# Grouped 1x1 convolution: one in-place ring in slots of 128 columns, with register addresses on TensorE

## The chip, the cores and the metric

The kernel runs on one core of a Trainium2 chip. The metric is device time in microseconds, from the first to the last instruction of one execution with what the launch adds around it. A profile is one execution recorded by the chip's profiler; its times are its own.

## What is computed

An image of 512 x 512 pixels has 192 channels in bf16, in 4 groups of 48. Each pixel's 48 channels of a group are multiplied by that group's 48 x 48 matrix; the kernel size is 1 and there is no padding.

```
H = W = 512; G = 4; Cg = 48; C = 192; k = 1
x: (1, 512, 512, 192) bf16        w: (1, 1, 4, 48, 48) bf16
out = einsum('bhwgc,gcd->bhwgd', x.reshape(B, H, W, G, Cg), w[0, 0])
return out.reshape(B, H, W, C)
```

The input is 100.66 MB and so is the output; both go through DMA once.

## The kernel before, in words

**Tiling.** The pixels are laid over the 128 partitions of SBUF, so that a *column* is one pixel of each partition, 192 channels or 384 bytes of a partition's row. Four columns are a *group*, two groups a *pair*. The plan makes 529 groups in 265 pairs.

**Pieces.** `plan_pieces` cuts the columns into slots of 64 (`SLOT`); the first slot is cut further into pieces of 8, 24 and 32 (`HEAD`). Two slots (`SHARED_AT`) are *shared* pieces that fill only 60 of the 128 partitions, so that one of the 16 DMA engines has less to move: 16 partitions go by the ordinary queues and 44 by GpSimd's. There are two rings in SBUF, `xin` and `xout`, of 256 columns each (four slots).

**Engines.** SyncE issues the transfer of the weights (L231) and then the load of each piece (L235), waiting before each until TensorE is done with the columns that it overwrites (`groups_before`, counted on `mm_done`). GpSimd builds an identity and a selection matrix, issues the shared pieces' second part (L204, L206; the small `cur` transfers turn its DMA engines round to the right one), and announces each landed piece to TensorE by adding its pairs to `ready` (L219). TensorE builds a block weight matrix from ten small matmuls (L247), which VectorE casts to `wt` (L306). Then for each pair it does 12 transposes (L261: six blocks of 128 x 128 per group, the input block being the operand that a weight load brings in and the identity the one that streams) and, one pair behind, 12 matmuls (L276) of the transposed data with `wt`. VectorE copies the transposes of a pair from PSUM to SBUF in one copy of 128 x 1536 (L312). ScalarE evicts each group's result to `xout` (L346, 128 x 768, f32 to bf16), waits first until the store that used these columns has landed, and issues the stores (L332) when a piece is complete; the last nine slots are stored in halves or quarters.

**Order on TensorE.** The order is written out by hand: transposes of pair j + 1, then matmuls of pair j. The matmuls wait for VectorE's copy by a semaphore step of the sequencer (L269, `e_left`) and, at the first matmul of each group, for an eviction of two groups earlier (`o_left`), since PSUM holds two groups of results. The loop (`Fori`, L288) has 64 groups in its body, as many as `xin` holds, so that every address is a constant. It turns 8 times; nine pairs follow it. At the end of a turn three semaphore steps (L292 to L294) lower the counters by one lap, and then an addition to the loop register and a branch follow (both L288). VectorE has a loop of the same length.

## Time and profile before

| what | us |
|---|---|
| three timed runs | 476.95, 484.16, 486.12 (median 484.16) |
| the profiled execution | 476.64, of it span 474.5 |
| TensorE busy (matmul, weight load) | 436.9, 394.1 |
| ScalarE busy | 398.4, of it 529 evictions at 802 ns |
| VectorE busy | 254.1 |
| data moved in the span | 201.53 MB, 425 GB/s in the mean |
| granted TensorE clock, mean | 0.981 |

Busy time of an engine is not its bound by itself: an engine can be busy nearly all the time at the pace of another. In the profile, PE is TensorE's matmul side and PEld its weight loads; a name with q (SPq, PEq, PEldq) is an engine's sequencer, for steps that use no datapath. `out<-in` names the tensors written and read. Idle time stands in brackets with what ended it; "issue" is idle time for which the profile shows no cause outside the engine.

### The profile page before, as it was taken

The numbers are of one execution on the slowest core, as the hardware profiler recorded it, in microseconds if no ns is written. First come the engines' busy times: TensorE is split into PE (matmuls) and PEld (weight loads), VectorE is DVE, ScalarE is ACT, GpSimd is POOL, SyncE is SP. The second block draws the span as 40 slices with busy tenths as digits, with TensorE's granted clock in tenths as the row PEclk, the third lists the DMA queues.
The fourth block names the chain that finished last, engine by engine and source line by source line (L and its number), as shares of the span: only waits on it lengthen the run. The fifth ranks groups of instructions, "written<-read, shape, count | busy, mean of one in ns | idle before, by whom it ended". The sixth has DMA issues, their size and how long they took to land.

```text
span 474.5 us, 14050 instructions
## 1 busy us (share of the span) xinstructions
PE 436.9 (92%) x6358; PEld 394.1 (83%) x6358; DVE 254.1 (54%) x266; ACT 398.4 (84%) x530; POOL 5.9 (1%) x16
## 2 busy tenths in 40 slices
PE   4999999999999999999889859999989999999970
PEld 4988988988989889898779759898879898988860
DVE  2556555555555555555555535555555555555540
ACT  2899989998999989998888848999879998998880
POOL 1000100000000000000000000000000000000000
PEclk9999999999999999999999979999999999999995
DMA  8999999999999999999999999999999999999998
GB/s 329 427 406 432 431 428 433 431 431 429 429 429 432 429 431 429 431 429 431 429 434 429 437 433 433 435 431 433 429 430 435 431 422 433 431 431 421 427 426 334
DMA packets 11981, 201.53 MB, mean 425 GB/s; under 512 B 1744, under 2 KB 2000, under 8 KB 2640
## 3 DMA queue, kind: packets, MB, share of 16 engines
q1 hardware_dynamic: 5144, 98.52, 48.6%
q10 hardware_dynamic: 6376, 98.50, 48.6%
q0 software_dynamic: 448, 4.33, 2.2%
q8 instruction: 8, 0.13, 0.1%
q14 instruction: 5, 0.04, 0.0%
HBM read 100.68 MB, written 100.66 MB: 424 GB/s over the span
## 4 chain that ended last, share of the span: by engine, by line
PE 56%; DMA 39%; ACT 1%; issue 1%; SPq 0%; POOLq 0%; ACTq 0%
PE o_ps L276 33%; PE xT_ps L261 23%; DMA xin<-in_x_dram 20%; DMA out_dram<-xout 18%; ACT xout L346 1%; SPq L235 0%; SPq L231 0%; POOLq L219 0%; ACTq L51 0%
## 5 line engine op out<-in xcount | busy, mean ns | idle before, releaser
L346 ACT CAST xout<-o_ps 128x768 bf16<-128x768 f32 x529 | 397.1, 802 | 62.1 <-PE o_ps L276 51.0
L312 DVE COPY xT_sb<-xT_ps 128x1536 bf16<-128x1536 bf16 x265 | 253.4, 956 | 201.3 <-PE xT_ps L261 201.3
L276 PE MATMUL o_ps<-wt,xT_sb 128*128 128x144 bf16 (+1 forms) x3174 | 294.3, 234 | 6.8 <-ACT xout L346 2.7
L276 PEld LDWEIGHTS o_ps<-wt,xT_sb 128*128 128x128 bf16 x3174 | 212.8, 98 | 46.8 <-ACT xout L346 30.6
L261 PE MATMUL xT_ps<-ident,xin 128*128 128x128 bf16 x3174 | 223.5, 221 | 14.0 <-POOLq L219 12.7
L261 PEld LDWEIGHTS xT_ps<-ident,xin 128*128 128x128 bf16 x3174 | 192.2, 99 | 16.6 <-POOLq L219 14.1
L204 POOL DMA_DIRECT2D cur<-in_x_dram x4 | 2.3, 584 | 321.0 <-PE o_ps L276 162.0
L247 PE MATMUL o_ps<-w_sb,esel 48*128 48x48 bf16 x10 | 0.6, 210 | 2.7 <-DMA w_sb<-in_w_dram 2.7
L247 PEld LDWEIGHTS o_ps<-w_sb,esel 48*128 48x128 bf16 x10 | 0.5, 113 | 2.7 <-POOL esel L190 2.7
L306 DVE CAST wt<-o_ps 128x480 bf16<-128x480 f32 x1 | 0.7, 658 | 3.3 <-PE o_ps L247 3.3
L346 ACT ACT_TABLE_LOAD x1 | 1.3, 1283 | 0.8 <-PEq L367 0.8
L206 POOL DMA_DIRECT2D xin<-in_x_dram x2 | 1.1, 563 | 0.0
L206 POOL DMA_DIRECT2D out_dram<-xout x2 | 1.1, 562 | 0.0
L190 POOL TENSOR_SCALAR_AFFINE_SELECT esel<-esel 48x272 bf16<-48x272 bf16 x1 | 0.4, 402 | 0.0
L187 POOL MEMSET esel<- 48x272 bf16 x1 | 0.3, 318 | 0.3 <-POOLq L367 0.3
L194 POOL TENSOR_SCALAR_AFFINE_SELECT ident<-ident 128x128 bf16<-128x128 bf16 x1 | 0.3, 282 | 0.0
L188 POOL MEMSET ident<- 128x128 bf16 x1 | 0.2, 198 | 0.0
L367 POOL MEMSET const-float32-0.0<- 128x1 f32 x1 | 0.1, 98 | 0.3 <-issue 0.3
L367 POOL MEMSET const-bfloat16-1.0<- 128x1 bf16 x1 | 0.1, 101 | 0.0
L367 POOL MEMSET const-uint8-127<- 128x1 uint8 x1 | 0.1, 101 | 0.0
L367 POOL MEMSET const-float32-1.0<- 128x1 f32 x1 | 0.1, 98 | 0.0
## 6 DMA issues: line engine op xcount, KB each, us to landing
xin<-in_x_dram SPq DMA_DIRECT2D x30, 3072.0 KB, 35.3
out_dram<-xout ACTq DMA_DIRECT2D x22, 3072.0 KB, 32.7
out_dram<-xout ACTq DMA_DIRECT2D x15, 1536.0 KB, 33.5
out_dram<-xout ACTq DMA_DIRECT2D x2, 1152.0 KB, 17.5
xin<-in_x_dram POOLq DMA_DIRECT2D x2, 1056.0 KB, 19.9
out_dram<-xout POOLq DMA_DIRECT2D x2, 1056.0 KB, 19.3
xin<-in_x_dram SPq DMA_DIRECT2D x1, 1536.0 KB, 9.4
xin<-in_x_dram SPq DMA_DIRECT2D x3, 384.0 KB, 3.5
```

Source lines behind the costliest of these rows:

```text
L187: gp.memset(esel[:], 1.0).then_inc(p0_sem, 1)
L190: gp.affine_select(out=esel[:], in_=esel[:], pattern=[[-1, ECOLS]], compare_op=AluOpType.is_equal, fill=0.0, base=ESHIFT, channel_multipli ...
L194: gp.affine_select(out=ident[:], in_=ident[:], pattern=[[-1, 128]], compare_op=AluOpType.is_equal, fill=0.0, base=0, channel_multiplier=1) ...
L204: gp.dma_start(cur[0:turn, turns[0]], few).then_inc(cur_sem, 16)
L206: gp.dma_start(*((sbuf, dram) if inward else (dram, sbuf))).then_inc(done, 16)
L247: last = pe.matmul(o_ps[:, NOB - 1, col:col + CG], lhsT=esel[:, s0:s0 + 128], rhs=w_sb[:, g, :], start=True, stop=True, skip_group_check=True)
L261: last = pe.transpose(xT_ps[:, g % NXP, i * 128:(i + 1) * 128], xg[:, i * 128:(i + 1) * 128], ident[:])
L276: last = pe.matmul(o_ps[:, v % NOB, c0_:c1_], lhsT=xs[:, i * 128:(i + 1) * 128], rhs=wt[:, WOFF[tc]:WOFF[tc] + (c1_ - c0_)], start=(tc == ...
L306: dve.tensor_copy(wt[:], o_ps[:, NOB - 1, 0:WCOLS]).then_inc(wc_sem, 1)
L312: dve.tensor_copy(xT_sb[pair % NXS][:, 0:n * 2 * UC].rearrange("p (g c) -> p g c", g=n), xT_ps[:, b0:b0 + n, 0:2 * UC]).then_inc(e_left, 1)
L346: act.copy(dst, o_ps[:, v % NOB:v % NOB + 2, 0:UC]).then_inc(o_left, 1)
L367: nc = _bacc.Bacc("TRN2", target_bir_lowering=False, num_devices=1)
```

## The change

One ring takes the place of the two. `ring` holds 512 columns in four slots of 128; a group is loaded into it, and ScalarE evicts the result to the same columns, from which it is stored. A load therefore waits until the stores of a lap before have landed (`wait_free`, on SyncE and on GpSimd), and ScalarE no longer waits for stores. The ring is declared in bytes (`U8`) and its slices are read as bf16.

The first slot is cut into 8, 24, 32 and 64; the shared pieces are still 64 columns wide, each followed by an ordinary piece of 64. Only the last three slots are stored in parts. Full-width loads become 20 transfers and stores 25.

TensorE's loop covers one slot, 32 groups, and turns 16 times. As the slot changes from turn to turn, the address of each transposed block is a register: at the head of a turn the byte offsets of the slot and of the next one are computed (`here`, `there`), and for each of the 12 transposes of a pair the built program has a register addition (`RegisterAlu`) and then the transpose with the register as address. In the built loop body these are 194 register operations and 2 fused ones beside 384 transposes and matmuls. The nine pairs after the loop and the first pair before it have constant addresses, as before. VectorE's loop has 16 copies instead of 32.

SyncE issues the load of the first piece ahead of the transfer of the weights.

```diff
-SLOT = 64
-IN_COLS = 4 * SLOT
-OUT_COLS = 4 * SLOT
-HEAD = (8, 24, 32)
-LATE = 9
-LAST_PARTS = (24, 16, 12, 12)
-LOOP = IN_COLS // 4
-SHARED_AT = (6, 22)
+SLOT = 128
+COLS = 4 * SLOT
+COL = 2 * C
+HEAD = (8, 24, 32, 64)
+LATE = 3
+LAST_PARTS = (28, 16, 12, 12)
+LOOP = SLOT // 4
+SHARED_AT = (4, 10)
-AHEAD = IN_COLS // SLOT - 2
+WIDE = 64
+AHEAD = 1
...
-        xin = es.enter_context(nc.sbuf_tensor("xin", [128, IN_COLS * C], BF16))
-        xout = es.enter_context(nc.sbuf_tensor("xout", [128, OUT_COLS * C], BF16))
+        ring = es.enter_context(nc.sbuf_tensor("ring", [128, COLS * COL], U8))
...
+        def wait_stored(wq, i):
+            p = stores[i][0]
+            wq.wait(st_sem[i], 16 * len(p.on(SYNC)))
+            if p in pooled:
+                wq.wait(ps_sem[p], pool_val[p])
+
+        def wait_free(wq, p):
+            lap = COLS // 4
+            for i in sorted({store_of[g - lap] for g in range(p.g0, p.g1) if g >= lap}):
+                wait_stored(wq, i)
...
                 if ahead in pooled:
-                    wq.wait(mm_done, groups_before(ahead))
-                    pool_dmas(ahead, xf, xin, True, pl_sem[ahead])
+                    wait_free(wq, ahead)
+                    pool_dmas(ahead, xf, True, pl_sem[ahead])
...
-            sp.dma_start(w_sb[:], wv).then_inc(w_sem, 16)
             for p in pieces:
-                wq.wait(mm_done, groups_before(p))
-                for _, dram, sbuf in transfers(xf, xin, p, SYNC):
+                wait_free(wq, p)
+                for _, dram, sbuf in transfers(xf, p, SYNC):
                     sp.dma_start(sbuf, dram).then_inc(ld_sem[p.i], 16)
+                if p.i == 0:
+                    sp.dma_start(w_sb[:], wv).then_inc(w_sem, 16)
...
-                    xg = columns(xin, g)
-                    for ul in range(2):
-                        for tc in range(3):
-                            i = ul * 3 + tc
-                            last = pe.transpose(xT_ps[:, g % NXP, i * 128:(i + 1) * 128],
-                                                xg[:, i * 128:(i + 1) * 128], ident[:])
+                    for i in range(6):
+                        at = 4 * g % SLOT * COL + i * 256
+                        if base is None:
+                            xs = ring[:, 4 * g % COLS * COL + i * 256:][:, 0:256]
+                        else:
+                            xs = ring[:, bass.ds(base + at, 256)]
+                        last = pe.transpose(xT_ps[:, g % NXP, i * 128:(i + 1) * 128], xs.bitcast(BF16), ident[:])
...
-                with pe.Fori(0, turns_of_loop):
+                with pe.Fori(0, turns_of_loop) as turn:
+                    here = pe.snap((turn & 3) * (SLOT * COL))
+                    there = pe.snap(((turn + 1) & 3) * (SLOT * COL))
                     for j in range(LP):
-                        transposes(j + 1, range(2 * j + 2, 2 * j + 4))
+                        transposes(j + 1, range(2 * j + 2, 2 * j + 4), here if j + 1 < LP else there)
                         matmuls(j, range(2 * j, 2 * j + 2))
...
             for g in range(NG):
-                if g >= OUT_COLS // 4:
-                    wait_stored(store_of[g - OUT_COLS // 4])
                 wq.wait(mm_done, g + 1)
                 v = 2 * g
-                dst = columns(xout, g).rearrange("p (u c) -> p u c", u=2)
+                dst = columns(g).rearrange("p (u c) -> p u c", u=2)
```

More of the change, by code (lines that the diff above doesn't have):

```diff
@@ L8 @@
 F32 = mybir.dt.float32
+U8 = mybir.dt.uint8
 GROUPS = 4
@@ L23 @@
 ECOLS = 272
-SLOT = 64
-IN_COLS = 4 * SLOT
-OUT_COLS = 4 * SLOT
-HEAD = (8, 24, 32)
-LATE = 9
-LAST_PARTS = (24, 16, 12, 12)
-LOOP = IN_COLS // 4
-SHARED_AT = (6, 22)
+SLOT = 128
[6 more added lines that the diff above has]
+SHARED_AT = (4, 10)
 SYNC, POOL = 0, 1
-SHARED = ((0, 16, 4, SLOT, SYNC), (52, 44, 11, SLOT, POOL))
-AHEAD = IN_COLS // SLOT - 2
+WIDE = 64
+SHARED = ((0, 16, 4, WIDE, SYNC), (52, 44, 11, WIDE, POOL))
+AHEAD = 1
 NXP = 4
@@ L64, in __init__ @@
         self.i, self.slot, self.size = i, slot, size
-        self.at = {IN_COLS: 4 * g0 % IN_COLS, OUT_COLS: 4 * g0 % OUT_COLS}
+        self.at = 4 * g0 % COLS
         self.g0, self.g1 = g0, g0 + size // 4
@@ L72, in __init__ @@
         self.pix_end = pix
-        assert size % 4 == 0 and all(at + size <= cols for cols, at in self.at.items())
+        assert size % 4 == 0 and self.at + size <= COLS
     def on(self, queue):
@@ L88, in plan_pieces @@
         if n in at:
-            parts = [(SLOT, SHARED)]
+            parts = [(WIDE, SHARED), (SLOT - WIDE, None)]
         elif n == 0 and cols >= SLOT:
@@ L122, in groups, with span, transfers @@
         return range(2 * pair, min(2 * pair + 2, NG))
-    def transfers(ap, ring, p, queue, c0=0, c1=None):
-        at = p.at[ring.shape[1] // C]
+    def span(c0, c1, r0=0, r1=128):
+        return ring[r0:r1, c0 * COL:c1 * COL].bitcast(BF16)
+    def transfers(ap, p, queue, c0=0, c1=None):
+        at = p.at
         for b in p.on(queue):
@@ L132, in transfers @@
                 view = px.rearrange("(c a i) n -> a c (i n)", a=b.parts, c=b.rows // b.parts)
-            yield b, view, ring[b.r0:b.r0 + b.rows, (at + e0) * C:(at + e1) * C]
+            yield b, view, span(at + e0, at + e1, b.r0, b.r0 + b.rows)
     stores = []
@@ L139, in bass_standalone__grouped__vision_kernel @@
         parts = (p.size,)
-        if p.full and p.size == SLOT and late < LATE:
-            parts = LAST_PARTS if late == 1 else (p.size - half, half)
+        if p is pieces[-1] and p.size == sum(LAST_PARTS):
+            parts = LAST_PARTS
+        elif p.full and late < LATE and half:
+            parts = (p.size - half, half)
         c = 0
@@ L174, in bass_standalone__grouped__vision_kernel, with columns @@
         ready, e_left, o_left = sem("ready"), sem("e_left"), sem("o_left")
-        def columns(ring, g):
-            c = 4 * g % (ring.shape[1] // C)
-            return ring[:, c * C:(c + 4) * C]
-        def groups_before(p):
-            pairs = (p.g1 - LOOP + 1) // 2
-            return max(2 * pairs - 3, pairs > 0)
+        def columns(g):
+            c = 4 * g % COLS
+            return span(c, c + 4)
+        def wait_stored(wq, i):
[7 more added lines that the diff above has]
+                wait_stored(wq, i)
         @block.gpsimd
@@ L197, in _, with pool_dmas @@
             cursor, turns = [0], [0]
-            def pool_dmas(p, ap, ring, inward, done):
-                for b, dram, sbuf in transfers(ap, ring, p, POOL):
+            def pool_dmas(p, ap, inward, done):
+                for b, dram, sbuf in transfers(ap, p, POOL):
                     turn = (b.engine - cursor[0]) % 16
@@ L222, in _ @@
                     wq.wait(mm_done, q.g1 + 2)
-                    pool_dmas(q, of, xout, False, ps_sem[q])
+                    pool_dmas(q, of, False, ps_sem[q])
             for p in pooled:
@@ L249, in build_weights, with transposes @@
                 last.then_inc(wb_sem, 1)
-            def transposes(j, gs):
+            def transposes(j, gs, base=None):
                 if j % LP in starts:
@@ L296, in _ @@
             for j in range(NP - first[0]):
-                g0 = 2 * first[0]
                 if j + 1 < NP - first[0]:
-                    transposes(j + 1, [g - g0 for g in groups(first[0] + j + 1)])
-                matmuls(j, [g - g0 for g in groups(first[0] + j)])
+                    transposes(j + 1, groups(first[0] + j + 1))
+                matmuls(j, [g - 2 * first[0] for g in groups(first[0] + j)])
         @block.vector
@@ L330, in store @@
                 p, c0, c1, g1 = todo.pop(0)
-                for _, dram, sbuf in transfers(of, xout, p, SYNC, c0, c1):
+                for _, dram, sbuf in transfers(of, p, SYNC, c0, c1):
                     act.dma_start(dram, sbuf).then_inc(st_sem[i], 16)
-            def wait_stored(i):
-                p = stores[i][0]
-                wq.wait(st_sem[i], 16 * len(p.on(SYNC)))
-                if p in pooled:
-                    wq.wait(ps_sem[p], pool_val[p])
             for g in range(NG):
-                if g >= OUT_COLS // 4:
-                    wait_stored(store_of[g - OUT_COLS // 4])
                 wq.wait(mm_done, g + 1)
                 v = 2 * g
-                dst = columns(xout, g).rearrange("p (u c) -> p u c", u=2)
+                dst = columns(g).rearrange("p (u c) -> p u c", u=2)
                 act.copy(dst, o_ps[:, v % NOB:v % NOB + 2, 0:UC]).then_inc(o_left, 1)
@@ L352, in _ @@
             for i in range(len(stores)):
-                wait_stored(i)
+                wait_stored(wq, i)
 _INS = ['x', 'w']
```

## The prediction, made before the changed kernel ran

> **What bounds the kernel now.** I read the page first (busy shares, slices, DMA queues), then the groups by line, the waits, SyncE's waits, the table by stage, and last the timeline around one back edge of TensorE's loop.

> ```profile
> PE 436.9 (92%) x6358; PEld 394.1 (83%) x6358; DVE 254.1 (54%) x266; ACT 398.4 (84%) x530; POOL 5.9 (1%) x16
> ...
> DMA  8999999999999999999999999999999999999998
> ...
> q1 hardware_dynamic: 5144, 98.52, 48.6%
> q10 hardware_dynamic: 6376, 98.50, 48.6%
> q0 software_dynamic: 448, 4.33, 2.2%
> ```

> The three data queues' packets take 48.6 + 48.6 + 2.2 = 99.4% of what 16 DMA engines have in the span: 472 of 474.5 us. Transfers are the bound from end to end; neither end has more than some 2 us of slack. But TensorE (92%) and ScalarE (84%) stand close behind.

> ```profile
> 60.00:230.00 170.00, 167.03 (x2461) 150.73 (x2459) 98.47 (x103) 153.78 (x206) 1.10 (x2) 1.00 1.00 430
> 230.00:290.00 60.00, 50.99 (x721) 45.75 (x719) 28.49 (x30) 44.84 (x61) 1.10 (x2) 0.94 1.00 431
> ```

> Columns: stretch, its length, busy us of PE, PEld, DVE, ACT, POOL, clock, DMA share, GB/s. From 60 to 230 us TensorE runs without a stall: 103 VectorE copies (one per pair of groups) in 170 us, 1.65 us a pair, working off what loads had brought early. After 230 us it waits for loads. So compute's own pace is 1.63 to 1.65 us a pair, while the DMA engines allow 472/265 = 1.78. The whole reserve of compute is about 0.13 us a pair, 34 us over 265 pairs.

> ```profile
> PEld o_ps L276 <- ACT xout L346: 30.6, 130, 0.2
> PE xT_ps L261 <- POOLq L219: 12.7, 7, 4.9
> ACT xout L346 <- DMA out_dram<-xout: 2.9, 2, 2.3
> ```

> The pace of 1.63 is ScalarE's: in every second group a weight load waits for an eviction. Now the place where TensorE's sequencer does steps of its own, between two turns of the loop:

> ```profile
> 167.68 0.39 PEld L276 LDWEIGHTS o_ps<-wt,xT_sb 128*128 128x128 bf16 x6 [0.24 <-ACT xout L346]
> 168.51 0.67 PEld L261 LDWEIGHTS xT_ps<-ident,xin 128*128 128x128 bf16 x12 [0.45 <-issue]
> ```
> ```profile
> L288 PEldq ALU_OP  x8: 36/36/42, 62.2 to 445.9; - x8
> L288 PEldq COMPARE_BRANCH  x8: 76/208/235, 62.4 to 446.0; - x8
> ```

> Between those weight loads stand three semaphore steps (L292 to L294), one ALU_OP and one branch: 0.83 us from the load that ScalarE released to the first transpose, five steps that TensorE could not hide. In the trace's records of this edge the three semaphore steps start 150 ns apart, the ALU_OP's successor 97 ns after it (97 to 102 over the eight turns), and the first semaphore step 14 ns after the release: a sequencer step begins only when the waiting weight load ahead of it has been released. This is the row that decides the case.

> **The change part by part.**

> *Larger transfers.* In the trace a 12288-byte packet takes 460 ns and a 24576-byte one 912: 8 ns fixed plus 27.2 GB/s, so 1816 for 49152 bytes. Full-width loads fall from 34 to 20 transfers of 128 packets, full-width stores from 44 to 25: 33 x 128 packets x 8 ns / 16 engines = 2.1 us, and 33 x 16 completion packets of 9 ns give 0.3. Lower bound of the gain 0 (rows split again), upper 2.4; taken: 2.4, since two sizes lie on one line.

> *Weights behind the first piece.* SyncE's issues are 0.45 us apart, so the first load starts 0.45 us sooner, worth that while DMA is the bound. The weight transfer (18 KB) passes behind the 384 KB piece: issued at 1.26 us, 1.8 us to land plus about 0.9 for the piece ahead, so near 4.0; the ten small matmuls end at 4.6, where the first transposes start at 4.8 now. Their VectorE cast (0.66) ends long before the loop at 8 us. Cost nothing; cover gone, at most 0.5 us.

> *In-place ring.* ScalarE loses its wait for stored columns (2.9 us in all); SyncE and GpSimd now wait for the stores of a lap before. Behind that wait on SyncE stand only later loads. A slot is 6.3 MB each way, 29 us at 215 GB/s; load 29, transposing and matmuls 16 pairs x 1.65 = 26, store 29, latencies 4: 88 us, against 4 slots x 29 = 117. The load queue keeps 29 us in hand, so nothing. GpSimd waits likewise before it announces the piece ahead of each of the two shared pieces; bounds 0 and 2 x 4.9 us (the longest wait of transposes on L219), taken 0 by the same margin.

> *Registers.* Each of the 12 transposes of a pair gets a register addition, 192 a turn over 16 turns; a turn also has four more address steps at its head, and there are 16 edges for 8. Nothing on an ordinary queue is moved; all of it goes in front of TensorE's weight loads, and VectorE, then ScalarE, wait for the transposes behind them. Call c the sequencer's time for one addition with its transpose. Low end: 36 (the ALU_OP itself) plus 10 (after an edge 24 static instructions went out in at most 123 ns, 5 each) = 46 ns. High end: the weight load with a register address is a sequencer step too: 97 + 97 + 10 = 204. Taken: 97 + 10 = 107, the only row for a register operation on this engine, and the trace has no dynamic load that says more.

> What c does: the additions of the next pair start when ScalarE has released the second group (time A). Then 12c for transposes, 0.09 to pass the semaphore step, 0.63 for six matmuls to ScalarE's start, 0.70 until ScalarE takes the second eviction, 0.80 for that one, 0.05 to the weight load it releases: 12c + 2.27 us, after which two pairs have gone by. So a pair takes 6c + 1.13, and the edge (five steps 0.83, four more 0.39) adds 1.2/16 = 0.08. For c = 107: 0.64 + 1.13 + 0.08 = 1.85 us, over both 1.63 and 1.78.

> [...]

> **Sum.** Profiled execution 476.64 us (span 474.5, 2.1 around it; the median of the three runs is 484.16, lowest 476.95, so it stands with the fastest). Loop entered at 8.0; 256 pairs x 1.85 = 473.6; 9 static pairs x 1.63 = 14.7; last eviction and store about 5.5 (0.8 + 0.3 + the 3.5 that a small load takes, and a little); 501.8, plus 2.1: **504 us**, 6% slower. The gains of 2.9 us on the DMA are not seen, as DMA is no longer the bound.

> **Rivals.**

> *A, additions hidden, DMA still the bound.* 476.6 - 2.4 - 0.45 = **473.7 us**. It needs c below (1.743 - 1.21)/6 = 89 ns. For it: the ALU_OP's own record is 36 ns, and on VectorE the same operation's successor comes after 72. Against: 97 on this engine, before the two engine instructions are added. From c = 95 on (486 us) it would be over 2% slower. Past the break-even each 10 ns of c are 256 x 0.06 = 15 us.

> *B, the forecast*: the additions pace TensorE, each transpose otherwise as cheap as before: c from 89 to 130 ns, 477 to 540 us.

> *C, the weight load with a register address is decoded step by step as well.* Then the additions alone pace the pair: 12 x 0.204 + 0.09 + 0.08 = 2.62 us, and 8 + 671 + 20 + 2 = **701 us**; if it costs only half as much again (c = 155), 2.14 us and 578. For it: no static load shows what a register does to it; against: nothing either, so I keep it.

> [...]

> *D, the ring starves the loads*: it decides if a slot's way exceeds 117 us, that is, a pair over (117 - 62)/16 = 3.4 us; no case above gets there.

> **How the numbers follow.** A 0.34 (471 to 477 us), B 0.40 (477 to 540, of it 0.07 below 486), C 0.25 (above 540), anything else 0.01. B is the likeliest and the forecast; the time is that of its row, 504, its own range 477 to 540. The range for 8 in 10 reaches down to A's 471 (its DMA gain may be 2 us larger) and up to 600, which leaves out the upper half of C. About 2% is what a measurement of this kernel can tell from no change, as its three runs spread over 1.9%. Faster by over 2% is a part of A alone, where the steadier transfers also avoid what made two of the three runs take 484 and 486: 0.08. Within 2%: the rest of A and B below 486, 0.34. Slower: 0.58.

> **What would show it.** Right: ALU_OP rows at the transposes' line, about 3,070; transposes' weight loads about 107 ns apart instead of 56; idle time before them put down to issue; DMA share falling below 9 tenths in the middle; 1.85 us between VectorE copies. Packets of 49152 bytes at 1816 ns and a first load at 0.8 us show the DMA steps. Wrong: copies 1.65 us apart while data are there and DMA full to the end (A), or transposes 150 ns and more apart (C).

## The result, and the profile after

The changed kernel takes 518.98 us (median of 4 runs, 518.64 to 519.11); the kernel before, run beside it, took 476.95 to 499.02 (median 485.14, 4 runs). The ratio is 1.0876, 95% interval 1.0862 to 1.0889: slower by 8.8%. The ratios, here and below, leave out executions that ran slower at a lower granted clock, which the medians and ranges still hold, so this one is a ratio to about 477 us, the time of the profiled execution on which the sum was made. The forecast was 504 us. The profiled execution after took 518.95 us, with a span of 517.4.

From the page of the changed kernel: the engines, the slices of the DMA engines, and the three data queues.

```profile
PE 494.4 (96%) x6358; PEld 439.6 (85%) x6358; DVE 254.1 (49%) x266; ACT 398.3 (77%) x530; POOL 5.9 (1%) x16
...
DMA  8999999899999989989999899999999999998547
...
q1 hardware_dynamic: 3128, 98.52, 46.6%
q10 hardware_dynamic: 3640, 98.50, 45.1%
q0 software_dynamic: 448, 4.33, 2.0%
```

The queues' packets now take 93.7% of the span, for 99.4% before, and the slices show holes from the eighth on and a long ebb at the end. ScalarE works as long as before (398 us), TensorE 58 us longer. DMA has stopped being the bound.

The table by stage of the changed kernel (stretch, its length, busy us and instructions of PE, PEld, DVE, ACT, POOL, then clock, DMA share, GB/s):

```profile
60.00:230.00 170.00, 166.95 (x2147) 148.61 (x2148) 85.73 (x90) 133.97 (x179) 2.37 (x4) 1.00 0.97 403
230.00:290.00 60.00, 58.94 (x761) 52.32 (x759) 29.95 (x32) 47.53 (x64) 1.11 (x2) 1.00 0.94 380
450.00:517.00 67.00, 59.53 (x786) 52.54 (x783) 31.21 (x33) 51.06 (x69) 0.00 (x0) 0.98 0.74 313
```

In the first stretch VectorE made 103 copies before and makes 90 now: 170/90 = 1.89 us a pair of groups for 1.65. The granted clock is 1.00 in this stretch of both. TensorE is "busy" in both, which is why this view alone would mislead: the record of a transpose's matmul is 219 ns long in both traces (median), so records that start 112 ns apart overlap as those 56 ns apart do, and leave no gap. The waits tell more (engine, tile and line, what was waited for, us in total, times, longest):

```profile
DVE xT_sb L328 <- PE xT_ps L277: 250.2, 265, 3.6
POOL cur L217 <- DMA out_dram<-ring: 172.4, 2, 104.1
...
ACT ring L354 <- PE o_ps L291: 103.1, 158, 9.4
PEld o_ps L291 <- ACT ring L354: 22.5, 107, 0.2
PEld xT_ps L277 <- issue: 13.6, 19, 3.3
...
PE xT_ps L277 <- POOLq L232: 3.5, 2, 3.0
```

VectorE and ScalarE both wait for TensorE; TensorE waits for data (GpSimd's announcement, L232) for 3.5 us in all, 12.7 before. The ring does not starve it. What TensorE's queue does in between stands at the transposes' line:

```profile
L277 PEldq ALU_OP  x3088: 32/32/42, 8.9 to 495.3; - x193
L277 PEldq FUSED_REGOPS  x32: 37/37/42, 9.0 to 494.0; - x32
```

The record of an addition is 32 ns long, yet in the trace the additions start 112 ns apart (111 to 113 in 2,430 of 3,087 steps): 60 ns from its start to its weight load, 52 to the next addition. The record's length is the wrong column to price it by. One round of the chain, two pairs long, from TensorE's weight loads in the timeline (start, busy us, line), and ScalarE's evictions in it:

```profile
113.34 0.38 PEld L291 LDWEIGHTS o_ps<-wt,xT_sb 128*128 128x128 bf16 x6 [0.24 <-ACT ring L354]
113.71 1.08 PEld L277 LDWEIGHTS xT_ps<-ident,ring 128*128 x12
114.82 0.81 PEld L291 LDWEIGHTS o_ps<-wt,xT_sb 128*128 128x128 bf16 x12
115.62 0.72 PEld L277 LDWEIGHTS xT_ps<-ident,ring 128*128 x12
116.40 0.40 PEld L291 LDWEIGHTS o_ps<-wt,xT_sb 128*128 128x128 bf16 x6
117.02 0.38 PEld L291 LDWEIGHTS o_ps<-wt,xT_sb 128*128 128x128 bf16 x6 [0.22 <-ACT ring L354]
```
```profile
113.35 1.50 ACT L354 CAST ring<-o_ps 128x768 bf16<-128x768 f32 x2
115.47 2.38 ACT L354 CAST ring<-o_ps 128x768 bf16<-128x768 f32 x3 [0.62 <-PE o_ps L291]
```

At 113.34 ScalarE releases the second group's matmuls. The next pair's twelve transposes end in the first matmul at 114.82, 1.48 us later; ScalarE starts on that at 115.47, makes two evictions in 1.50 (the third of the row starts at 117.05) and releases the next second group at 117.02: 1.48 + 0.65 + 1.50 + 0.05 = 3.68 us for two pairs. The other twelve transposes of the round (115.62) go out within 0.72 us: in the trace their additions run from 114.91 to 116.19, beside the twelve matmuls at 114.82 and ScalarE's two evictions, so they are done before ScalarE's release at 117.02.

### The profile page after: what moved, and what is told of

Same layout as the page of the kernel before. It is cut to its first block, busy times and chain, and to the rows that moved or that the text cites. A ratio compares the mean times of both kernels' runs of the same rounds, so it can differ in the third digit from the quotient of the medians.

```text
span 517.4 us, 17180 instructions
## 1 busy us (share of the span) xinstructions
PE 494.4 (96%) x6358; PEld 439.6 (85%) x6358; DVE 254.1 (49%) x266; ACT 398.3 (77%) x530; POOL 5.9 (1%) x16
## 3 DMA queue, kind: packets, MB, share of 16 engines
q1 hardware_dynamic: 3128, 98.52, 46.6%
q10 hardware_dynamic: 3640, 98.50, 45.1%
q0 software_dynamic: 448, 4.33, 2.0%
## 4 chain that ended last, share of the span: by engine, by line
PE 84%; DMA 13%; issue 2%; ACT 1%; SPq 0%; POOLq 0%
PE o_ps L291 44%; PE xT_ps L277 40%; DMA ring<-in_x_dram 7%; DMA out_dram<-ring 6%; ACT ring L354 1%; SPq L249 0%; SPq L247 0%; POOLq L232 0%
## 5 line engine op out<-in xcount | busy, mean ns | idle before, releaser
L354 ACT CAST ring<-o_ps 128x768 bf16<-128x768 f32 x529 | 397.0, 802 | 112.4 <-PE o_ps L291 103.1
L277 PE MATMUL xT_ps<-ident,ring 128*128 128x128 bf16 x3174 | 275.7, 219 | 9.9 <-issue 6.4
L291 PE MATMUL o_ps<-wt,xT_sb 128*128 128x144 bf16 (+1 forms) x3174 | 281.7, 233 | 2.2 <-issue 0.4
L277 PEld LDWEIGHTS xT_ps<-ident,ring 128*128 (+1 forms) x3174 | 231.1, 97 | 32.0 <-issue 13.6
L261 PE MATMUL o_ps<-w_sb,esel 48*128 48x48 bf16 x10 | 0.6, 209 | 4.2 <-DMA w_sb<-in_w_dram 4.2
L261 PEld LDWEIGHTS o_ps<-w_sb,esel 48*128 48x128 bf16 x10 | 0.4, 111 | 4.1 <-issue 4.1
L219 POOL DMA_DIRECT2D ring<-in_x_dram x2 | 1.1, 566 | 0.0
L219 POOL DMA_DIRECT2D out_dram<-ring x2 | 1.1, 562 | 0.0
```

Of the source, the lines that this page charges most:

```text
L219: gp.dma_start(*((sbuf, dram) if inward else (dram, sbuf))).then_inc(done, 16)
L261: last = pe.matmul(o_ps[:, NOB - 1, col:col + CG], lhsT=esel[:, s0:s0 + 128], rhs=w_sb[:, g, :], start=True, stop=True, skip_group_check=True)
L277: last = pe.transpose(xT_ps[:, g % NXP, i * 128:(i + 1) * 128], xs.bitcast(BF16), ident[:])
L291: last = pe.matmul(o_ps[:, v % NOB, c0_:c1_], lhsT=xs[:, i * 128:(i + 1) * 128], rhs=wt[:, WOFF[tc]:WOFF[tc] + (c1_ - c0_)], start=(tc == ...
L354: act.copy(dst, o_ps[:, v % NOB:v % NOB + 2, 0:UC]).then_inc(o_left, 1)
```

## The experiments

The experiments ran on more than one chip; each ratio is to runs of the kernel before on the same chip.

**Registers alone, on the kernel before.** Two rings of 256, slots of 64, weights first, all as before; the transposes in the loop take their address from a register.

```
-LOOP = IN_COLS // 4
+LOOP = IN_COLS // 8
...
+                            if base is not None:
+                                at = (4 * g % (IN_COLS // 2) * C + i * 128) * 2
+                                xb = xraw[:, bass.ds(base + at, 256)].bitcast(BF16)
...
+                    here = pe.snap((turn & 1) * half)
+                    there = pe.snap(((turn + 1) & 1) * half)
```

> The kernel before with register addresses alone: both rings of 256 columns, slots of 64 and the weights' place stay; the loop body holds 32 groups (half the input ring) for 64, so 16 turns with 12 additions a pair, as in the changed kernel. Theory S (TensorE's sequencer: a transpose with its addition takes 112 ns and a pair 1.83 us, plus about 1 us at each of 16 edges): about as slow as the changed kernel, 8 + 16 x 30.35 + 21 + 2 = 517 us, range 505 to 522. Theory R (the in-place ring or the wider slots starve the loads): 475 to 480, as before.

Measured: 516.16 us (515.68 to 516.74), ratio 1.077 [1.069, 1.085]. Its stage from 60 to 230 us:

```profile
60.00:230.00 170.00, 166.47 (x2141) 147.62 (x2139) 85.52 (x90) 133.81 (x179) 1.10 (x2) 1.00 0.99 412
```

Again 90 copies, with neither the in-place ring nor the wide slots. The additions start 112 ns apart here too. Theory S holds, theory R falls: registers alone carry all but about 3 us of the change's cost (5 by the ratios).

**The operation without the address.** One register operation ahead of each transpose; the transposes' addresses stay constants, so that the price of the operation is seen apart from that of a weight load with a register address.

```
+            def toggle():
+                pe.reg_alu(spare, spare, 256, AluOpType.bitwise_xor)
...
+                            if add:
+                                toggle()
```

> The kernel before with one register operation ahead of each transpose in the loop, whose result no transpose of the loop uses: all addresses stay constants, 8 turns of 64 groups. Theory S (the operation itself costs the sequencer about 112 ns, wherever its result goes): a pair takes 1.83 us, 9 + 8 x (32 x 1.83 + 0.7) + 21 + 2 = 506 us, range 498 to 512. Theory L (the price lies with the weight load whose address is in a register, the operation being only its own record of 32 ns): below 1.63 us a pair, so 475 to 480.

Measured: 569.71 us (566.69 to 570.76), far above both. Two things are in it. Between the loop's edges a pair takes 1.88 us (median of the eight turns, without the first pairs of each), near the 1.83 of theory S: in this stage 27 copies in 50 us,

```profile
84.00:134.00 50.00, 49.72 (x644) 45.01 (x642) 25.86 (x27) 39.99 (x54) 1.10 (x2) 1.00 0.92 370
```

and the operations again start 112 ns apart. So the operation itself has the price, and the weight load with a register address adds none that these runs can show. The rest is at the edges, which the expectation had at 0.7 us; TensorE's weight loads around the first of them:

```profile
68.51 0.81 PEld L288 LDWEIGHTS o_ps<-wt,xT_sb 128*128 128x128 bf16 x12
77.87 1.38 PEld L274 LDWEIGHTS xT_ps<-ident,xin 128*128 128x128 bf16 x12 [8.55 <-issue]
```

8.55 us in which the engine waited for nothing that the profile shows. What differs besides is the page's row for instruction packets:

```profile
q8 instruction: 73, 1.20, 0.8%
```

73 packets of 16 KB, about nine a turn; the kernel before has 8 in the whole run. This reads as a longer body that is fetched anew at each turn, which the expectation did not foresee and its 506 us leave out.

**TensorE's order.** The changed kernel, with half of a pair's transposes put between the two groups of matmuls, two pairs ahead.

```
+                            first_group(j, 2 * j)
+                            transposes(j + 2, range(2 * j + 4, 2 * j + 6), here if j + 2 < LP else there,
+                                       lambda: second_group(j, range(2 * j, 2 * j + 2)))
```

> The changed kernel with TensorE's order in the loop changed alone: the first group's matmuls of pair j, the first six transposes of pair j+2, the second group's matmuls, the other six transposes. Six additions then stand in the time in which TensorE waits for ScalarE anyway, and VectorE has a whole pair in hand. Theory S (only additions between ScalarE's release and its next eviction count): ScalarE's 1.63 us a pair is the pace again, under the DMA's 1.78, so DMA is the bound: 476.6 - 2.4 - 0.45 = 473.7 us, range 470 to 480. Theory T (each addition takes its time out of TensorE wherever it stands, 12 x 0.112 for the transposes and 12 x 0.056 for the matmuls = 2.02 us a pair): 8 + 256 x 2.02 + 22 = 547 us.

Measured: 483.12 us (480.33 to 490.61, 12 runs), ratio 1.008 [1.004, 1.013]. From its page:

```profile
PE 438.1 (91%) x6358; PEld 416.2 (86%) x6358; DVE 254.1 (53%) x266; ACT 411.7 (85%) x530; POOL 5.9 (1%) x16
...
DMA  8999999999999999999999999999999999999995
...
q1 hardware_dynamic: 3128, 98.52, 48.3%
q10 hardware_dynamic: 3640, 98.50, 48.0%
q0 software_dynamic: 448, 4.33, 2.1%
```

The same 3,072 additions no longer set the pace: within a turn a pair takes 1.56 us, less than before, and packets fill 98.4% of the span. Theory T (547 us) falls: where an addition stands decides here, not how many there are; the twelve of a pair are 12 x 0.112 = 1.34 us of the sequencer's time, still less than 1.56. Some 36 us come back, though not the 45 of the expectation. The packets take 474.8 us an engine in the trace for 472.7 before, where the larger ones should have brought 470; and some 7 us of the span, most of them at its start and its end, are not filled. With DMA the bound, the waits on GpSimd that the prediction had at nothing reappear in the order's waits:

```profile
PE xT_ps L279 <- POOLq L232: 19.5, 4, 11.2
```

They cost no time while the DMA slices stay full around them (the longest, 11.2 us, ends at 320 us of the span, where the slices are at 9).

**An in-place ring without registers.** 256 columns, slots of 64, a loop body of a whole lap of 64 groups with constant addresses.

```
-SLOT = 128
+SLOT = 64
...
-LOOP = SLOT // 4
+LOOP = COLS // 4
...
-                with pe.Fori(0, turns_of_loop) as turn:
-                    here = pe.snap((turn & 3) * (SLOT * COL))
-                    there = pe.snap(((turn + 1) & 3) * (SLOT * COL))
+                with pe.Fori(0, turns_of_loop):
```

> The in-place ring without registers: one ring of 256 columns (half the SBUF of the two rings before), slots of 64, weights behind the first piece, the loop body a whole lap of 64 groups with constant addresses, 8 turns. Theory S: no addition, so DMA stays the bound: 476.6 - 0.45 = 476, range 473 to 480. Theory R (an in-place ring makes loads wait for stores): a ring of half the depth should then be as slow as the changed kernel or slower, 500 us and more.

Measured: 487.31 us (485.48 to 488.45), ratio 1.016 [1.010, 1.022]. Neither theory's number: no 500, but 1.6% over before. TensorE's waits and the chain that ended last of this kernel:

```profile
PE xT_ps L277 <- POOLq L232: 28.7, 18, 3.2
```

```profile
DMA 66%; PE 30%; ACT 1%; issue 1%; SPq 0%; POOLq 0%
```

Eighteen short waits for data, up to 3.2 us, for seven in the kernel before. But DMA leads the chain, and its packets fill 98.3% of the span and take some 5 us an engine more than before, so the waits stand beside a DMA that is nearly full. That a shallow ring makes loads wait for the stores of the lap before, and that this is what the 1.6% pay for, is likely but not shown; it says nothing against 512 columns.

**The changed ring and slots, constant addresses.** A body of a whole lap of 512 columns, 128 groups, four turns: `LOOP = COLS // 4`, and the transposes without a base as in the run above.

> The changed kernel with constant addresses in place of register addresses, so the loop body holds a whole lap of 128 groups and is gone through 4 times; in-place ring of 512 columns and slots of 128 stay. Theory S: without additions a pair takes 1.65 us and DMA is the bound, 472 to 480 us, if no instructions have to be fetched. With fetching (the kernel before with idle register operations, whose body was about a quarter longer than that of the kernel before, stood still for 8 to 11 us at each of its 7 edges): 3 edges x 10 to 17 us, which the ring of 512 hides up to its 29 us in hand, so 475 to 500 us. Theory R (ring or slots cost the time): 510 us and more even between the edges, that is, over 1.8 us a pair with data in the ring.

Measured: 492.51 us (486.38 to 498.93), ratio 1.021 [1.013, 1.028]. A stage between two edges, TensorE's waits, and the instruction queue:

```profile
150.00:230.00 80.00, 79.66 (x1176) 71.76 (x1174) 46.84 (x49) 73.23 (x99) 0.00 (x0) 1.00 1.00 429
```

```profile
PE xT_ps L277 <- issue: 24.3, 6, 8.3
```

```profile
q8 instruction: 56, 0.92, 0.7%
```

49 copies in 80 us, 1.63 a pair, with the DMA share at 1.00: neither the ring nor the slots slow compute. What the trace shows besides are three edges of 9.6 to 10.8 us from copy to copy, with instructions fetched in 56 packets. That they keep the kernel at 492, the ring hiding a part of them only, is argued and not tested; the data packets fill 97.0% of its span, which leaves 14.7 us.

**Two operations more, in two places.** Both on the changed kernel: two register operations a pair, once among the first group's matmuls (ahead of the wait for ScalarE), once among the second's (behind ScalarE's release).

```
+                            if looping[0] and g % 2 == 0 and i in (1, 3):
+                                toggle()
```

The second kernel has `g % 2 == 1` there.

> The changed kernel with two more register operations a pair, put among the matmuls of the pair's first group, ahead of the wait for ScalarE that the second group's matmuls have; their result is used by no instruction of the loop. Theory S, chain (an addition counts where it stands between ScalarE's release and the next eviction): 519 to 525 us. Theory T, throughput (each costs the sequencer 112 ns wherever it stands): 519 + 256 x 0.224 = 576 us.

> As the run with two operations among the first group's matmuls, but among those of the second group, behind ScalarE's release and ahead of the next pair's transposes. Theory S, chain: they lie on the way once in two pairs, 519 + 256 x 0.112 = 548 us, range 540 to 580, and over 15 us more than with the same two operations in the first group. Theory T, throughput: 576 us, the same as there.

Measured: 522.38 us (521.81 to 523.53) in the first place, 549.82 (548.02 to 550.09) in the second. The stages from 60 to 230 us, first place, then second:

```profile
60.00:230.00 170.00, 167.77 (x2127) 152.72 (x2127) 84.81 (x89) 132.75 (x179) 2.36 (x4) 1.00 0.97 401
```

```profile
60.00:230.00 170.00, 167.29 (x2026) 150.59 (x2026) 80.92 (x85) 126.01 (x168) 2.36 (x4) 1.00 0.95 391
```

The same operations cost 3.4 us in one place and 30.8 in the other, for 0 to 6 and 29 expected; 576 would have been the time if each took its 112 ns wherever it stands. A turn takes 30.61 us with them in the first place and 32.33 in the second, for 30.36 without. This is the sharpest of the runs: the chain over two pairs is right. In the second place 1.97 us a turn, over eight rounds with two operations on the chain in each, are 0.12 us for one of them, near the 112 ns of its distance.

**Eight operations for twelve.** The kernel before with idle operations, none ahead of the third and the sixth transpose of a group.

```
-                            if add:
+                            if add and i in (0, 1, 3, 4):
```

> As the kernel before with an idle register operation ahead of each transpose, but with eight a pair in place of twelve (none ahead of the third and sixth transpose of a group). Theory S, chain: two pairs take 8 x 0.112 + 2.31 = 3.21 us, so a pair 1.60 us, which is ScalarE's own 1.63: the operations are hidden and DMA is the bound, 476 to 482 us, if the shorter body (some 1,830 instructions for 1,960) is not fetched again at each turn; if it is, about 9 us more at each of 7 edges, of which the ring hides a part, 490 to 540 us, with copies 1.65 us apart between the edges all the same. Theory T, throughput (each operation costs its 112 ns): (8 x 0.112 + 4 x 0.056 + 12 x 0.056) = 1.79 us a pair between the edges, about 490 us without fetching.

Measured: 529.06 us (524.39 to 530.78): the body is still fetched anew (72 packets; 8.9 to 9.8 us from copy to copy at the edges). Between the edges a pair takes 1.69 us (median of the turns), 0.19 less than with twelve. Theory S had 1.63, T 1.79; the run lies nearer S, and the 0.06 in between is left open.

**The weights first again**, on the changed kernel: the issue of the weights' transfer goes back ahead of SyncE's loop over pieces.

```
+            sp.dma_start(w_sb[:], wv).then_inc(w_sem, 16)
             for p in pieces:
...
-                if p.i == 0:
-                    sp.dma_start(w_sb[:], wv).then_inc(w_sem, 16)
```

> The changed kernel with the weights' transfer issued first again, ahead of the first piece; nothing else is altered. Theory W (behind the first piece, the small transfer makes the second piece land late: 8.87 us after the start for 7.95, and the weights themselves are there 1.5 us later; the kernel before with register addresses, its weights first, ended its first turn 2.3 us sooner): 519.0 - 2.3 = 516.7 us, range 516 to 517.5. Theory S as the prediction had it (the place of the weights costs nothing; the ring and the wider slots make the late start): 519 us, range 518.4 to 519.6.

Measured: 517.78 us (516.99 to 518.60, 6 runs) for 518.98. All six lie below all four of the changed kernel, on another chip: about 1.2 us, half of what theory W had. In the profile the second VectorE copy comes 3.12 us after the first, for 4.54 in the changed kernel, and the first turn ends at 39.7 us for 41.0. All the traces together lean the same way: with the weights behind the first piece the second piece is announced 8.80 to 9.26 us after the start in five of six, with the weights first 7.34 to 8.00 in all seven. The sixth is the run with two operations among the first group's matmuls: announced at 7.64, second copy after 3.50 us, first turn ended at 40.0. So the weights' place probably makes the second piece late; the exception keeps the 1.2 us from being settled as its price.

**Two versions that might have been better.** The new order with the weights first, and the new order on the kernel before (the edit of the second):

```
+                    transposes(1, range(2, 4))
...
+                            transposes(j + 2, range(2 * j + 4, 2 * j + 6),
+                                       lambda: second_group(j, range(2 * j, 2 * j + 2)))
```

> The changed kernel with TensorE's new order (first group's matmuls, six transposes, second group's matmuls, six transposes) and the weights' transfer first again. Theory W: the start gains 1 to 2 us, and as DMA is the bound in that order the whole run does, 483 - 1.5 = 481.5, range 480 to 483. Theory S: no difference from the same order with the weights behind, 483.

> The kernel before (constant addresses, two rings, weights first) with TensorE's new order in its loop, as a version that may beat both. If DMA bounds the kernel before from end to end, a faster pair on TensorE is worth nothing: 476 to 479 us, the same as before. If the pair's 1.65 us is what lets some of its runs take 480 us and more, the median falls by 1 to 4 us and the spread shrinks.

Measured: 488.60 us (479.56 to 494.42, 8 runs), ratio 1.010 [1.007, 1.013], and 485.05 us (476.40 to 489.98, 6 runs). By the ratios the first is no better than the order alone (1.008). The second's lowest run is level with that of the kernel before on the same chip (476.29), and its runs spread as widely (476.29 to 488.46 there); no gain can be seen. With DMA the bound, TensorE's new order brought nothing here, and no version beat the kernel before.

## Why the prediction was right in its mechanism and short in its size

**What bounds.** Right: DMA bounded the kernel before, with a reserve of compute of about 0.13 us a pair. With the additions a pair takes 1.83 within a turn, 0.19 more than the 1.64 of that kernel's turns, so the bound changed hands.

**The price of an addition.** 107 ns were taken, 112 measured. That it was read from one ALU_OP's successor in the loop's edge, not from its own 36 ns, is what made the step hold. Of its two parts, 97 for the step and 10 for the two instructions behind it, the second was the short one: at the head of a turn, where nothing stands between, a register operation's successor starts 96 to 97 ns after it, so the two instructions take 15 to 16. Rival A needed under 89 ns; rival C, a weight load with a register address decoded step by step, is refuted by the same 112 ns with constant addresses.

**The chain.** Right in shape, shown by the two places (3.4 and 30.8 us) and by the new order (483 us). Its terms were 12c + 0.09 = 1.37, 0.63, 1.50 and 0.05, in sum 3.55 us for two pairs; the round above has 1.48, 0.65, 1.50 and 0.05, in sum 3.68, and the mean over turns is 3.66.

**Where the 15 us are.** The step that failed is a size: the term "256 pairs x 1.85" of the sum, where the trace has 1.90 us a pair. A turn of 16 pairs takes 30.35 us from branch to branch, for 29.6: 16 x 0.06 = 0.96 more for the pairs, 0.21 less for the edge (1.07 for 1.28). Of the 0.06 about half is c. Most of the rest is additions that do not keep to the 112: in the round above two of them start 128 and 143 ns after the one before, which the sum, with one c for all twelve, had no room for. Fifteen such turns are 11.2 us. The first turn ended at 41.0 us for 37.6 (8.0 + 29.6): 3.4 us, of which 0.75 are that turn's pace and about 2.6 the start. The end took 0.8 more, what lies around the span 0.5 less: 14.9 in all. A term that counts 256 times leaves no room: 0.05 us a pair are 13 us.

**The start.** "Cost nothing; cover gone, at most 0.5 us" was wrong for the weights. They landed 2.8 us after their issue, as forecast; missed was the second piece behind them in the same queue, announced at 8.87 us for 7.95. The run with the weights first puts the price at about 1.2 us; with registers alone, weights first and the old rings, the first turn ended 2.3 us sooner. How the late start divides between the weights' place, the ring and the slots stays open.

**Ring and GpSimd's waits at nothing.** Right for this kernel, by the 3.5 us of waits for data and the runs with constant addresses. The cover named was 29 us of load queue in hand; with half the ring, 28.7 us of waits appear and the time is 1.6% longer, though how much of that the waits make is open.

**Larger packets.** The duration was right (1816 ns forecast, median 1815 in the trace); the gain of 2.4 us is not seen even where DMA is the bound again: in the new order's trace the mean of these packets is 1841 ns for loads and 1844 for stores, and the sum over all packets is 2.1 us larger than before, not smaller. A median that fits does not make a sum.

**Instructions beside an addition.** Weight loads that stand ahead of an addition in the program start beside it: in the new order the six of one group start from 112.32 to 112.62 us, and three additions for the next transposes between 112.37 and 112.64. Those behind the additions, where nothing else holds them, follow one addition each: in the changed kernel the twelve of a pair that start from 102.42 us on are 112 or 113 ns apart in nine of eleven steps. So a time near what DMA allows comes with the order in which the additions stand ahead of a wait (483), and not with the one that was made (519).

## What to carry to other kernels

Price a register operation on TensorE by the distance to its successor in the trace (here 112 ns), not by its record (32 ns), and then ask where it stands: between a release by ScalarE and the next matmul that ScalarE waits for it counts in full (here 30.8 us for two a pair), ahead of a wait it counts almost nothing (3.4 us). Before an address goes into a register to shorten a loop body, see whether the order of the instructions can put the additions into an existing wait; here that alone gave back 36 of 42 us. Where DMA is the bound, put the reserve of the next engine beside the change's cost per pair, since a few ns an addition, six times in a pair's chain and over 256 pairs, are what decides.
